# The low half of g on VectorE in the second feed-forward, and four blocks of w_out split in the last expert

## The chip, the core and the metric

The kernel runs on one NeuronCore of a Trainium2 chip. Its engines run side by side, each with an in-order queue: TensorE (PE, with weight loads as PEld), VectorE (DVE), ScalarE (ACT), GpSimd (POOL) and SyncE (SP, which issues DMAs). They wait for one another by semaphores. The metric is the device time of one execution in microseconds (us); the median of three runs of the kernel before is 1164.04 us (1163.69 to 1168.49).

## The reference

Three stages follow one another on 3072 tokens of width 384. A recurrence over time with decaying states (4 sequences, 8 heads, 768 tokens of 48 numbers a head) gives `x`. A mixture of 8 experts sends each token to the two with the largest noisy logits. The third stage, the second feed-forward, is where the change lies:

```python
def _moe2_ref(x, w_in, w_out) -> np.ndarray:
    h = x @ w_in            # 384 -> 2048
    g = h - np.tanh(h)
    return (g @ w_out).astype(np.float32)   # 2048 -> 384
```

## The kernel before

The first two stages end near 731 us of the span. The order of all instructions is written out by hand: each engine executes its own in the order in which the program issues them, and nothing moves them.

To keep precision, a matrix product is made from three: each factor is split into a high half (rounded to the type that TensorE reads, by a ScalarE copy) and a low half (the factor minus its high half), and high x high, high x low and low x high are summed in PSUM. So every operand of TensorE costs a copy and a subtraction: for `w_out` in `split_o` (L996, copy L999, subtraction L1001), for the tokens `x2h` and `x2l` in `x2_t` (L979, L980), for `g` in `split_g` (gh L1054, gl L1055).

`ff2` (L1009) takes six blocks of 512 tokens; a block is sixteen steps, one for each 128 columns of `w_in`. In step i:

- `l1` (L1022) makes h in PSUM (tile `tp`, three buffers) with nine matmuls of 512 columns. ScalarE takes t = h^2, tanh h, two shifted squares s0 and s1, and a mask m for small h (L1031 to L1039). VectorE takes s0 (L1041), s1 (L1042, reads PSUM), th = h - tanh h (L1043, reads PSUM), g from the polynomial s0 * s1 (L1044), and copies th over g where the mask says so (L1047). Between L1044 and L1047 it runs whatever waits in the list `fill`.
- `split_g` (L1050) of step i - 1: gh on ScalarE, gl on GpSimd.
- `l2` (L1060) of step i - 3 (LAG = 3): twelve matmuls of 384 columns that add g's product with a block of `w_out` into four accumulators.

Beside this, in the first five blocks, the tokens of the next block are prepared: `gather2` at f = 0, 2, 4, 6 issues two indirect DMAs on GpSimd (L951) that fetch a tile's two rows from `y_dram` into `yg`; `combine` at f = 3, 5, 7, 9 scales one on GpSimd (L961) and puts the add (L964) into `fill`; `x2_t` at f = 12, 13, 14 transposes on TensorE and splits. The tiles `yg` have two buffers each, so the third gather waits for the first add.

`w_out` has sixteen blocks of 128 rows. The first eight (NPS = 8) are split during the experts. The other eight are split in the first block of `ff2`, at f in SPLIT (L1076): the copy on ScalarE ahead of the step, the subtraction into `fill`. In the last expert (e = 7) the loop of `experts` runs its sixteen steps s with `combine` on ScalarE at s = 12 to 15 for the first four tiles, whose gathers it issues at s = 10 to 13.

Of the kernel before, what the change touches and what calls it, by code (L numbers as in the profile page):

```python
# [11 lines left out]
F32 = mybir.dt.float32  # L12
# [10 lines left out]
NT, DM = B * S, H * D          # tokens, model width  # L23
NE, FF = 8, 1024               # experts, their hidden width
FF2 = 2048
KD = DM // 128                 # 3 blocks of the model width
C = 128                        # tokens in a chunk
NCH = S // C                   # chunks of a sequence
NTILE = NT // 128
NFB, NFB2 = FF // 128, FF2 // 128  # L30
PH = 4                         # pairs of heads
HW = H * 4 * D
FILL = 512                     # slots of expert 0 that the chunks before the last fill
CAP = 832                      # slots of an expert; slot number: position * NE + expert
P_MIN = 2.0 ** -63.5
W_LO, W_HI = 0.71, 1.4         # decays whose product over a chunk stays in (2^-64, 2^64): what Ln takes

NPS = 8                        # blocks of w_out split ahead of the second feed-forward

# (h - tanh h) / h^3 = GC * ((t + GA0)^2 + GB0) * ((t + GA1)^2 + GB1) with t = h^2 <= G_T  # L40
G_T = 0.36
# [5 lines left out]
class Kernel:  # L47
# [13 lines left out]
    # ------------------------------------------------------------------ constants  # L61
    def setup(self):
        V, A, G, SP = self.V, self.A, self.G, self.SP
        dp = self.pool(self.ctx, "dram", space=bass.MemoryType.DRAM)
        self.d_dram = dp.tile([S, B * H], F32, name="d_dram")
        self.x_dram = dp.tile([NT, DM], F32, name="x_dram")      # rows: chunk, batch, token
        self.y_dram = dp.tile([NE * CAP, DM], F32, name="y_dram")
        cs = self.cs = self.pool(self.ctx, "const")
        self.ps = self.pool(self.ctx, "psum", space=bass.MemoryType.PSUM)
        self.ident = cs.tile([128, 128], F32, name="ident")  # L70
        make_identity(self.nc, self.ident)
        self.slots = cs.tile([128, NTILE, 2], I32, name="slots")
        self.mx = cs.tile([128, NTILE, 8], F32, name="mx")
        self.run = cs.tile([128, NE], F32, name="run")
        self.flag = cs.tile([128, 1], I32, name="flag")
        self.nov = cs.tile([128, NE + 1], I32, name="nov")
        self.cnt = cs.tile([128, NE], F32, name="cnt")
        self.idx = cs.tile([128, 7 * NE], F32, name="idx")
        self.ix0 = cs.tile([128, FILL // 128], I32, name="ix0")
        self.ix = cs.tile([128, 7, NE], I32, name="ix")  # L80
        self.XTT, self.XG, self.RAW = {}, {}, {}
# [4 lines left out]
    def setup_gate(self, cs):  # L86
        """What routing needs."""
        V, G, SP, I = self.V, self.G, self.SP, self.I
        self.wgn = cs.tile([128, KD, 32], F32, name="wgn")
        V.memset(self.wgn[:, :, 16:32], 0.0)  # L90
        SP.dma_start(self.wgn[:, :, 0:8], I["moe_w_gate"].rearrange("(k p) e -> p k e", p=128))
        SP.dma_start(self.wgn[:, :, 8:16], I["moe_w_noise"].rearrange("(k p) e -> p k e", p=128))
        self.noise = cs.tile([128, NTILE, NE], F32, name="noise")
        for b in range(B):
            SP.dma_start(self.noise.rearrange("p (c b) e -> p c b e", b=B)[:, :, b, :],
                         I["moe_noise"][b * S:(b + 1) * S, :].rearrange("(c p) e -> p c e", p=128))
        self.tok = cs.tile([128, NTILE], I32, name="tok")
        G.iota(self.tok, pattern=[[128, NTILE]], base=0, channel_multiplier=1)
        self.tokf = cs.tile([128, NTILE], F32, name="tokf")
        V.tensor_copy(self.tokf, self.tok)  # L100
        self.row = cs.tile([128, 128], F32, name="row")
        G.iota(self.row, pattern=[[1, 128]], base=0, channel_multiplier=0,
               allow_small_or_imprecise_dtypes=True)
        self.iota8 = cs.tile([128, NE], F32, name="iota8")
        G.iota(self.iota8, pattern=[[1, NE]], base=0, channel_multiplier=0,
               allow_small_or_imprecise_dtypes=True)
        self.ltri = cs.tile([128, 128], F32, name="ltri")
        V.tensor_scalar(self.ltri, self.jp, 0.0, None, op0=OP.is_gt)
        self.rst = cs.tile([128, NE, B + 1], F32, name="rst")
        V.memset(self.rst, 1.0)  # L110
        V.memset(self.rst[:, :, 0:1], 0.0)
        self.ones = cs.tile([128, 128], F32, name="ones")
        V.memset(self.ones, 1.0)
        self.gate_reset()

    # ------------------------------------------------------------------ routing
# [4 lines left out]
    def gate_x(self, xs, b, again):  # L121
        """x^T of a tile of tokens, and its products with both gate matrices."""
# [7 lines left out]
    def gate_mm(self):  # L130
        """Transposed logits, a batch in each quadrant."""
# [8 lines left out]
    def gate_act(self):  # L140
        """ln(1 + exp(-|z|)), its exponential made exact by its logarithm."""
# [14 lines left out]
    def gate_top(self, c):  # L156
        """One-hot rows of the two experts with the largest noisy logits."""
# [27 lines left out]
    def gate_rank(self):  # L185
        """How many earlier tokens chose each expert."""
# [6 lines left out]
    def gate_slots(self, c, oh):  # L193
        """Slots of a chunk's choices, and its part of the table of tokens by slot: a product of
        one-hot rows (slot position modulo 128) and columns (position over 128, expert)."""
# [37 lines left out]
    def gate_fill(self):  # L233
        """After the chunks before the last: the last one's tokens get no slot among the first FILL of
        expert 0, so that these are final now."""
# [9 lines left out]
    def gate(self, c, part, again=False):  # L245
        """The routing of a chunk, in eight parts."""
# [21 lines left out]
    def finish_counts(self):  # L268
        """Tokens of each expert; the tiles of tokens to look at for those with more than CAP."""
# [9 lines left out]
    # ------------------------------------------------------------------ attention  # L279
    def attention(self, ctx):  # L280
# [73 lines left out]
        def s_lay(nm, n):  # L354
            """Into tiles padded to 64 a head; of w what it lacks to W_HI, and no less than 0 (exact for
            w from W_HI / 2 on)."""
# [162 lines left out]
        def units(n, lag):  # L519
            """Where the diagonal's part of the pipeline stands: two units a step until it runs ahead."""  # L520
            m = n + lag
            return [u for u in ((2 * m, 2 * m + 1) if m < 3 else (m + 3,)) if 0 <= u < NU]
# [33 lines left out]
    def recurrence(self, ctx):  # L556
        """Attention step by step, for decays of any size, and its routing."""
# [47 lines left out]
    # ------------------------------------------------------------------ experts  # L605
    def overflow(self, ctx):
        """Tokens past CAP of an expert: each takes a slot that another expert leaves free (there
        are more slots than choices), and its row is computed here, from all tokens."""
# [49 lines left out]
        # where a tile's row for an expert goes; past the end: nowhere  # L658
# [42 lines left out]
    def conv_load(self, cv, j):  # L701
        """A block of w_in or w_out as float64 words."""
# [9 lines left out]
    def convert(self, cv, dst):  # L712
        """float64 words (low, high) of [128, 384] elements to float32, cut toward zero; below
        float32's normal range: 0."""
# [31 lines left out]
    def experts(self, ctx):  # L746
# [53 lines left out]
        def l2(e, part, f):  # L800
            """The last 64 slots take both parts of h side by side: half of its rows each."""
# [32 lines left out]
        for i in range(len(steps) + LAG):  # L834
            if i < len(steps):
# [29 lines left out]
                if e == NE - 1:  # L865
                    if s == 8:
# [32 lines left out]
    # ------------------------------------------------------------------ second feed-forward  # L899
# [26 lines left out]
    def weights(self):  # L926
        """The softmax over the two chosen logits, its maximum taken off: exp(0) and exp(l2 - l1)."""
# [17 lines left out]
    def gather2(self, i):  # L945
        """The two rows of a tile's tokens; the first chunk's lie below 512 in each expert."""
# [35 lines left out]
    def x2_first(self):  # L982
        """The first block, with the tile that comes last done last."""
# [12 lines left out]
    def split_o(self, pool, f, late=None):  # L996
        h = pool.tile([128, DM], F32R, name=f"woh{f}")
        l = pool.tile([128, DM], F32R, name=f"wol{f}")
# [10 lines left out]
    def ff2(self, ctx):  # L1009
# [12 lines left out]
        def l1(j, f):  # L1022
# [20 lines left out]
            V.tensor_tensor(th, p, th, op=OP.subtract)  # L1043
            V.scalar_tensor_tensor(g, s0, GC, s1, op0=OP.mult, op1=OP.mult)  # L1044
# [5 lines left out]
        def split_g(j, f):  # L1050
# [4 lines left out]
            G.tensor_tensor(gl, g, gh.bitcast(F32), op=OP.subtract)  # L1055
# [20 lines left out]
        SPLIT = (0, 1, 2, 4, 6, 8, 10, 11)  # L1076
        LAG = 3
        steps = [(j, f) for j in range(NB) for f in range(NFB2)]
        for i in range(len(steps) + LAG):
            if i < len(steps):  # L1080
                j, f = steps[i]
                if j == 0 and f in SPLIT:
                    self.split_o(wp, NPS + SPLIT.index(f), fill)
# [7 lines left out]
                l1(j, f)  # L1091
            if 0 < i <= len(steps):
                split_g(*steps[i - 1])
# [3 lines left out]
    # ------------------------------------------------------------------ all of it  # L1097
# [51 lines left out]
```

## Time and profile before

| what | value |
|---|---|
| median of the runs | 1164.04 us |
| profiled execution, span from first to last instruction | 1161.4 us |
| PE busy | 1084.2 us, 93% |
| DVE busy | 845.0 us, 73% |
| ACT busy | 686.2 us, 59% |
| POOL busy | 513.8 us, 44% |
| POOL gl (L1055), 96 operations | 124.5 us, 1297 ns each |
| DVE g (L1044), 96 operations | 139.5 us, 1453 ns each |

The page lists the busy time of the whole span; the stages differ, so the stretches of the second feed-forward are read apart from the rest. For the profiled execution the page gives its span only; the time of a run is measured from outside and is some 2.6 us longer than that span in the median. A matmul's end is modelled, so successive starts say more of PE than its busy share.

### The profile page before, as it was taken

What the parts mean: (1) busy time and instruction counts of PE and PEld (TensorE: products, weight loads), DVE (VectorE), ACT (ScalarE), POOL (GpSimd) and SP (SyncE); (2) the same over time, 40 slices, a digit from 0 to 9 for tenths busy, and PEclk for the clock granted to TensorE, in tenths of its full rate; (3) what the DMA queues carried; (4) which work ended last, traced back from release to release, by engine and by line L of the source; (5) the groups of instructions that cost most, each with busy time, mean ns of one, the idle gap of its engine ahead of it and who ended that gap; (6) DMA issues with size and microseconds to landing.
All of it is one profiled execution on the core that took longest, in us unless ns stands there. A gap on an engine that the chain in (4) does not pass through costs nothing. (4 is left out here: it accounts for less than half of the span.)

```text
span 1161.4 us, 18339 instructions
## 1 busy us (share of the span) xinstructions
PE 1084.2 (93%) x6540; PEld 978.8 (84%) x6541; DVE 845.0 (73%) x1562; ACT 686.2 (59%) x1316; POOL 513.8 (44%) x487
## 2 busy tenths in 40 slices
PE   3788889769999999999999999989999999999997
PEld 2677778657989898989898989778988899888896
DVE  3789898835546465646554532799999999999995
ACT  5565666332535353535343432878888888888885
POOL 4687788413133323333323202463736556363332
PEclk9898899869999999999999999999999999999999
DMA  8965452233435344444354302100202011020000
GB/s 149 160 122 116 78 103 56 69 98 99 151 115 165 101 153 134 129 130 146 114 158 135 116 22 80 54 21 14 69 1 69 15 51 32 10 73 1 28 1 27
DMA packets 116719, 97.78 MB, mean 84 GB/s; under 512 B 39432, under 2 KB 109832, under 8 KB 116616
## 3 DMA queue, kind: packets, MB, share of 16 engines
q1 hardware_dynamic: 110088, 76.82, 25.2%
q0 software_dynamic: 6528, 19.67, 5.8%
q8 instruction: 54, 0.88, 0.3%
q14 instruction: 49, 0.40, 0.1%
HBM read 76.70 MB, written 19.76 MB: 83 GB/s over the span
## 5 line engine op out<-in xcount | busy, mean ns | idle before, releaser
L794 DVE SCALAR_TENSOR_TENSOR hb<-tp,hb 128x256 fp32r<-128x256 f32 (+1 forms) x192 | 79.7, 442 | 200.4 <-ACT hb L792 193.8
L792 ACT ACTIVATE hb<-tp 128x320 fp32r<-128x320 f32 (+1 forms) x128 | 66.2, 517 | 239.3 <-PE tp L789 212.3
L1055 POOL TENSOR_TENSOR gl<-g,gh 128x512 fp32r<-128x512 f32 x96 | 124.5, 1297 | 187.5 <-ACT gh L1054 182.9
L809 PE MATMUL sc<-wh,hb 128*128 128x384 f32 x512 | 156.5, 346 | 0.0
L1044 DVE SCALAR_TENSOR_TENSOR g<-s,s 128x512 f32<-128x512 f32 x96 | 139.5, 1453 | 1.0 <-POOL gl L1055 1.0
L725 POOL TENSOR_SCALAR cvm<-cvm 128x384 f32<-128x384 f32 x32 | 40.6, 1269 | 221.1 <-ACT cvm L724 221.1
L789 PE MATMUL tp<-xh,wl 128*128 128x512 f32 (+1 forms) x384 | 135.8, 354 | 0.0
L789 PE MATMUL tp<-xl,wh 128*128 128x512 f32 (+1 forms) x384 | 135.0, 352 | 0.0
L789 PE MATMUL tp<-xh,wh 128*128 128x512 f32 (+1 forms) x384 | 134.7, 351 | 0.0
L1028 PE MATMUL tp<-x2h,wih 128*128 128x512 f32 x288 | 115.4, 401 | 1.4 <-ACTq L1117 1.4
L1028 PE MATMUL tp<-x2l,wih 128*128 128x512 f32 x288 | 114.3, 397 | 0.0
L1028 PE MATMUL tp<-x2h,wil 128*128 128x512 f32 x288 | 114.3, 397 | 0.0
L951 POOL DMA_INDIRECT yg<-y_dram,slots x48 | 57.2, 1191 | 91.0 <-DMA y_dram<-yo 56.8
L809 PEld LDWEIGHTS sc<-wh,hb 128*128 128x128 f32 x512 | 94.7, 188 | 3.2
L809 PE MATMUL sc<-wl,hb 128*128 128x384 f32 x256 | 86.4, 338 | 0.0
L1031 ACT ACTIVATE t<-tp 128x512 f32<-128x512 f32 x96 | 57.3, 597 | 42.6 <-PE tp L1028 42.1
L1047 DVE COPY_PREDICATED g<-m,th 128x512 f32<-128x512 int32 x96 | 77.1, 803 | 7.4 <-ACT s L1037 0.5
L789 PEld LDWEIGHTS tp<-xh,wl 128*128 128x128 f32 x384 | 72.2, 188 | 8.0
L789 PEld LDWEIGHTS tp<-xh,wh 128*128 128x128 f32 x384 | 72.3, 188 | 6.3 <-DVE xl L781 0.4
L789 PEld LDWEIGHTS tp<-xl,wh 128*128 128x128 f32 x384 | 72.2, 188 | 6.2
L764 DVE TENSOR_TENSOR wl<-r,wh 128x384 fp32r<-128x384 f32 x128 | 71.5, 586 | 7.3 <-ACT wh L763 7.3
L1054 ACT ACTIVATE gh<-g 128x512 fp32r<-128x512 f32 x96 | 60.5, 630 | 27.1 <-DVE g L1047 14.2
(230 smaller groups left out, 2994.3 us busy)
## 6 DMA issues: line engine op xcount, KB each, us to landing
r<-in_moe_w SPq DMA_DIRECT2D x128, 192.0 KB
y_dram<-yo SPq DMA_DIRECT2D x48, 192.0 KB
raw<-in_moe_w_in SPq DMA_DIRECT2D x16, 384.0 KB
raw<-in_moe_w_out SPq DMA_DIRECT2D x16, 384.0 KB
nv<-in_v SPq DMA_DIRECT2D x6, 768.0 KB
x_dram<-xs SPq DMA_DIRECT2D x6, 768.0 KB
out<-o SPq DMA_DIRECT2D x24, 192.0 KB
nw<-in_w SPq DMA_DIRECT2D x20, 192.0 KB
```

Source lines behind the costliest of these rows:

```text
L764: V.tensor_tensor(WL[i, f], raw, WH[i, f].bitcast(F32), op=OP.subtract)
L789: T.matmul(p[:, :n], lhsT=w[0, f][:, k, :], rhs=x[part][:, k, :], start=q == 0, stop=q == 8)
L792: A.activation(hb[:, :n], p[:, :n], AF.Relu)
L794: V.scalar_tensor_tensor(hb[:, o:o + c1 - c0], p[:, c0:c1], 0.0, hb[:, c0:c1].bitcast(F32), op0=OP.max, op1=OP.subtract)
L809: T.matmul(ACC[j][:, :DM], lhsT=h, rhs=w[1, f], start=f == 0 and i == 0, stop=f == NFB - 1 and i == len(prods) - 1)
L951: self.G.indirect_dma_start(out=y, out_offset=None, in_=rows, in_offset=bass.IndirectOffsetOnAxis(ap=self.slots[:, i, j:j + 1], axis=0))
L1028: T.matmul(p, lhsT=w[:, k, :], rhs=x[j][:, k, :], start=q == 0, stop=q == 8)
L1031: A.activation(t, p, AF.Square)
L1044: V.scalar_tensor_tensor(g, s0, GC, s1, op0=OP.mult, op1=OP.mult)
L1047: V.copy_predicated(g, m.bitcast(I32), th)
L1054: A.activation(gh, g, AF.Copy)
L1055: G.tensor_tensor(gl, g, gh.bitcast(F32), op=OP.subtract)
```

## The change

It does two things. First, gl goes from GpSimd to VectorE: `l1` takes the step before as an argument and issues its `split_g` between L1043 and L1044. Second, blocks 8 to 11 of `w_out` (NPE = 4) are split in the last expert, at s = 11 to 14, into tiles of that expert's weights for f = 0 and 1, which no later matmul reads; `ff2` splits the remaining four at f = 2, 4, 6, 8. The rest of the edit takes comments out, so later lines move by up to ten.

```diff
+NPE = 4
...
                 if e == NE - 1:
+                    if s >= 11 and s - 11 < NPE:
+                        f0, i0 = divmod(s - 11, 2)
+                        self.split_o(None, NPS + s - 11, homes=(WH[i0, f0], WL[i0, f0]))
...
-    def split_o(self, pool, f, late=None):
-        h = pool.tile([128, DM], F32R, name=f"woh{f}")
-        l = pool.tile([128, DM], F32R, name=f"wol{f}")
+    def split_o(self, pool, f, late=None, homes=None):
+        if homes is None:
+            h = pool.tile([128, DM], F32R, name=f"woh{f}")
+            l = pool.tile([128, DM], F32R, name=f"wol{f}")
+        else:
+            h, l = (x if len(x.shape) == 2 else x.rearrange("p k x -> p (k x)") for x in homes)
...
-        def l1(j, f):
+        def l1(j, f, last):
...
             V.tensor_tensor(th, p, th, op=OP.subtract)
+            if last is not None:
+                split_g(*last)
             V.scalar_tensor_tensor(g, s0, GC, s1, op0=OP.mult, op1=OP.mult)
...
-            G.tensor_tensor(gl, g, gh.bitcast(F32), op=OP.subtract)
+            V.tensor_tensor(gl, g, gh.bitcast(F32), op=OP.subtract)
...
-        SPLIT = (0, 1, 2, 4, 6, 8, 10, 11)
+        SPLIT = (2, 4, 6, 8)
...
-                    self.split_o(wp, NPS + SPLIT.index(f), fill)
+                    self.split_o(wp, NPS + NPE + SPLIT.index(f), fill)
...
-                l1(j, f)
-            if 0 < i <= len(steps):
-                split_g(*steps[i - 1])
+                l1(j, f, steps[i - 1] if i else None)
+            elif i == len(steps):
+                split_g(*steps[-1])
```

VectorE's queue in the first two steps of `ff2`, before (s0, s1, th, g, the low half wol of a block of `w_out`, the predicated copy into g):

```order
L1041 SCALAR_TENSOR_TENSOR s_9215<-s_9215,t 128x512
L1042 SCALAR_TENSOR_TENSOR s_9217<-s_9217,tp 128x512
L1043 TENSOR_TENSOR th<-tp,th 128x512
L1044 SCALAR_TENSOR_TENSOR g<-s_9215,s_9217 128x512
L1001 TENSOR_TENSOR wol_9195<-wo_7475,woh_9194 128x384
L1047 COPY_PREDICATED g<-m,th 128x512
L1041 SCALAR_TENSOR_TENSOR s_9245<-s_9245,t 128x512
L1042 SCALAR_TENSOR_TENSOR s_9247<-s_9247,tp 128x512
L1043 TENSOR_TENSOR th<-tp,th 128x512
L1044 SCALAR_TENSOR_TENSOR g<-s_9245,s_9247 128x512
L1001 TENSOR_TENSOR wol_9229<-wo_7576,woh_9228 128x384
L1047 COPY_PREDICATED g<-m,th 128x512
```

and now:

```order
L1049 SCALAR_TENSOR_TENSOR s_9220<-s_9220,t 128x512
L1050 SCALAR_TENSOR_TENSOR s_9222<-s_9222,tp 128x512
L1051 TENSOR_TENSOR th<-tp,th 128x512
L1054 SCALAR_TENSOR_TENSOR g<-s_9220,s_9222 128x512
L1057 COPY_PREDICATED g<-m,th 128x512
L1049 SCALAR_TENSOR_TENSOR s_9246<-s_9246,t 128x512
L1050 SCALAR_TENSOR_TENSOR s_9248<-s_9248,tp 128x512
L1051 TENSOR_TENSOR th<-tp,th 128x512
L1065 TENSOR_TENSOR gl<-g,gh 128x512
L1054 SCALAR_TENSOR_TENSOR g<-s_9246,s_9248 128x512
L1057 COPY_PREDICATED g<-m,th 128x512
```

The two wol are gone from these steps, and from the second step on gl of the step before stands between th and g.

POOL's queue in the first block of `ff2`, before (DMA yg: the indirect DMAs of a gather; TENSOR_SCALAR yg: the scaling of a combine):

```order
L951 DMA yg_9197<-y_dram,slots 128x384
L951 DMA yg_9199<-y_dram,slots 128x384
L1055 TENSOR_TENSOR gl<-g,gh 128x512
L951 DMA yg_9265<-y_dram,slots 128x384
L951 DMA yg_9267<-y_dram,slots 128x384
L1055 TENSOR_TENSOR gl<-g,gh 128x512
L961 TENSOR_SCALAR yg_9197<-yg_9197,wt 128x384
L1055 TENSOR_TENSOR gl<-g,gh 128x512
L951 DMA yg_9352<-y_dram,slots 128x384
L951 DMA yg_9354<-y_dram,slots 128x384
L1055 TENSOR_TENSOR gl<-g,gh 128x512
L961 TENSOR_SCALAR yg_9265<-yg_9265,wt 128x384
```

and now:

```order
L955 DMA yg_9202<-y_dram,slots 128x384
L955 DMA yg_9204<-y_dram,slots 128x384
L955 DMA yg_9265<-y_dram,slots 128x384
L955 DMA yg_9267<-y_dram,slots 128x384
L965 TENSOR_SCALAR yg_9202<-yg_9202,wt 128x384
L955 DMA yg_9352<-y_dram,slots 128x384
L955 DMA yg_9354<-y_dram,slots 128x384
L965 TENSOR_SCALAR yg_9265<-yg_9265,wt 128x384
L955 DMA yg_9447<-y_dram,slots 128x384
L955 DMA yg_9449<-y_dram,slots 128x384
L965 TENSOR_SCALAR yg_9352<-yg_9352,wt 128x384
L965 TENSOR_SCALAR yg_9447<-yg_9447,wt 128x384
```

Only gathers and scalings are left; the second tile's gather follows the first one's at once, and each later gather still follows the scaling of an earlier tile.

ScalarE's queue in the last expert, at s = 10 to 14, before (hb: the high half of h; yg: the scaling of a combine, which waits for gathered rows):

```order
L792 ACTIVATE hb<-tp 128x320 x2
L959 ACTIVATE yg_8791<-yg_8791,wt 128x384
L792 ACTIVATE hb<-tp 128x320
L959 ACTIVATE yg_8820<-yg_8820,wt 128x384
L792 ACTIVATE hb<-tp 128x320
L959 ACTIVATE yg_8849<-yg_8849,wt 128x384
L792 ACTIVATE hb<-tp 128x320
```

and now (wh: the high half of a block of `w_out`, in a place of the expert's weights):

```order
L793 ACTIVATE hb<-tp 128x320
L1006 ACTIVATE wh_0_8273<-wo_7475 128x384
L793 ACTIVATE hb<-tp 128x320
L1006 ACTIVATE wh_0_8275<-wo_7576 128x384
L963 ACTIVATE yg_8791<-yg_8791,wt 128x384
L793 ACTIVATE hb<-tp 128x320
L1006 ACTIVATE wh_1_8316<-wo_7702 128x384
L963 ACTIVATE yg_8822<-yg_8822,wt 128x384
L793 ACTIVATE hb<-tp 128x320
L1006 ACTIVATE wh_1_8318<-wo_7831 128x384
L963 ACTIVATE yg_8853<-yg_8853,wt 128x384
L793 ACTIVATE hb<-tp 128x320
```

One copy stands behind each hb from s = 10 on, three of them ahead of a scaling.

## Rows read from the trace of the kernel before

**Rows 1.** The page, part 1: busy us, share of span, instructions of each engine.

```profile
PE 1084.2 (93%) x6540; PEld 978.8 (84%) x6541; DVE 845.0 (73%) x1562; ACT 686.2 (59%) x1316; POOL 513.8 (44%) x487
```

**Rows 2.** Windows: stretch, its length, busy us per engine, granted clock, DMA share, GB/s.

```profile
768.00:773.00 5.00, 5.00 (x18) 4.43 (x18) 3.93 (x6) 1.61 (x3) 3.12 (x3) 0.66 0.02 5
...
789.00:858.10 69.10, 68.56 (x348) 61.65 (x348) 67.46 (x88) 58.20 (x104) 37.66 (x28) 1.00 0.11 35
```

**Rows 3.** Waits in 732 to 1162: who waits for whom, us, times, longest.

```profile
PE sc L1068 <- POOL gl L1055: 5.8, 5, 3.4
...
PE g L59 <- DVE x2l L980: 1.9, 5, 0.5
...
PE sc L1068 <- ACT gh L1054: 0.4, 1, 0.4
```

**Rows 4.** Timeline, 761 to 770: start us, us, engine, line, operation, [idle before].

```profile
763.24 0.67 DVE L1044 SCALAR_TENSOR_TENSOR g<-s,s 128x512 f32<-128x512 f32 x1
763.33 3.10 POOL L951 DMA_INDIRECT yg<-y_dram,slots  x1 [0.31 <-issue]
...
765.53 0.67 DVE L1042 SCALAR_TENSOR_TENSOR s<-s,tp 128x512 f32<-128x512 f32 x1
...
767.78 0.44 PE L1068 MATMUL sc<-woh,gl 128*128 128x384 f32 x1 [3.38 <-POOL gl L1055]
...
769.52 1.64 DVE L964 SCALAR_TENSOR_TENSOR x<-yg,wt,yg 128x384 f32<-128x384 f32 x1 [1.07 <-POOL yg L961]
```

**Rows 5.** Groups of DVE and POOL, 732 to 1100: count, busy us, mean ns.

```profile
L1044 DVE SCALAR_TENSOR_TENSOR g<-s,s 128x512 f32<-128x512 f32 x84 | 120.6, 1436 | 1.0 <-POOL gl L1055 1.0
...
L951 POOL DMA_INDIRECT yg<-y_dram,slots x40 | 49.4, 1236 | 31.5 <-DVE x L964 13.5 <-ACT th L1033 10.6 <-issue 5.2
L961 POOL TENSOR_SCALAR yg<-yg,wt 128x384 f32<-128x384 f32 x20 | 35.3, 1763 | 0.0
```

**Rows 6.** Timeline of the stage's start, 737 to 748.

```profile
737.53 0.68 DVE L1044 SCALAR_TENSOR_TENSOR g<-s,s 128x512 f32<-128x512 f32 x1
...
738.13 0.55 DVE L1001 TENSOR_TENSOR wol<-wo,woh 128x384 fp32r<-128x384 f32 x1
...
738.60 0.76 DVE L1047 COPY_PREDICATED g<-m,th 128x512 f32<-128x512 int32 x1
...
739.25 0.67 DVE L1041 SCALAR_TENSOR_TENSOR s<-s,t 128x512 f32<-128x512 f32 x1
...
740.01 0.63 ACT L1054 ACTIVATE gh<-g 128x512 fp32r<-128x512 f32 x1
...
742.05 0.44 PE L1068 MATMUL sc<-woh,gl 128*128 128x384 f32 x1 [0.73 <-POOL gl L1055]
...
747.36 1.05 DVE L1047 COPY_PREDICATED g<-m,th 128x512 f32<-128x512 int32 x1
```

**Rows 7.** Timeline of the last steps, 1145 to 1153.

```profile
1145.63 0.68 DVE L1041 SCALAR_TENSOR_TENSOR s<-s,t 128x512 f32<-128x512 f32 x1
...
1147.23 1.29 POOL L1055 TENSOR_TENSOR gl<-g,gh 128x512 fp32r<-128x512 f32 x1 [2.92 <-ACT gh L1054]
...
1147.42 1.65 DVE L1044 SCALAR_TENSOR_TENSOR g<-s,s 128x512 f32<-128x512 f32 x1
...
1148.57 0.44 PE L1068 MATMUL sc<-woh,gl 128*128 128x384 f32 x1 [0.36 <-POOL gl L1055]
...
1149.17 0.76 DVE L1047 COPY_PREDICATED g<-m,th 128x512 f32<-128x512 int32 x1
...
1150.02 0.63 ACT L1054 ACTIVATE gh<-g 128x512 fp32r<-128x512 f32 x1 [2.86 <-DVE g L1047]
...
1150.73 1.27 POOL L1055 TENSOR_TENSOR gl<-g,gh 128x512 fp32r<-128x512 f32 x1 [2.21 <-ACT gh L1054]
...
1152.05 0.44 PE L1068 MATMUL sc<-woh,gl 128*128 128x384 f32 x1 [0.73 <-POOL gl L1055]
```

**Rows 8.** Waits of the last expert's end, 700 to 730.

```profile
ACT yg L959 <- DMA yg<-y_dram,slots: 8.9, 4, 3.7
```

## The prediction

> **What bounds the kernel now.** I read the page's busy line first: PE is busy 93% of the span and DVE 73% [rows 1]. That mean hides the second feed-forward (the last 420 us), so I read its stretches next. From 789.00 to 858.10, one block of sixteen steps, PE is busy 68.56 of 69.10 us and DVE 67.46 [rows 2]. Both look full, so I asked the list of waits who really waits. In all of this stage PE stopped 5 times for POOL's gl, 5.8 us in total with one stop of 3.4, 5 times for VectorE's x2l, 1.9 us, and once for ScalarE's gh, 0.4 us [rows 3]. PE therefore bounds the steady blocks, and their matmuls can't be shortened by this change; what can be won is those stops and what follows from them.
>
> Where do the stops lie? Two of the five for gl are at the very end (0.36 and 0.73 us [rows 7]), the other three in the first block: 5.8 - 1.09 = 4.7 us. The largest is shown in the rows of 761 to 770 us. POOL began an indirect DMA at 763.33 and needed 3.10 us for it, where 1.24 us is the mean of the forty in this stage [rows 4, 5]; gl stood behind it in POOL's queue, and PE went on at 767.78 after 3.38 us of waiting. Then the clock fell: from 768 to 773 the granted clock was 0.66, so part of that stretch ran at the lower of PE's two levels, 1.2 instead of 2.4 GHz, behind the longest idle time of the stage [rows 2].
>
> DVE's 97% is mostly not work. Its operation g takes 1.44 us in the mean [rows 5] but 0.68 while POOL does nothing [rows 6]. The last steps show why: gl runs on POOL from 1147.23 to 1148.52, g is issued at 1147.42 and ends at 1149.07, 0.55 after gl. It sits out gl, then does its own work [rows 7].
>
> The profiled span is 1161.4 us; the median of the runs is 1164.0, so 2.6 us lie around the span. I take differences from the span and subtract them from the median.
>
> **gl on VectorE.** Removed: 96 POOL operations of about 1.3 us. Added: 96 VectorE operations of the same size. The trace has no gl on VectorE. The nearest row is g without POOL beside it, 0.68 us with two SBUF operands of the same shape [rows 6]. VectorE starts its operations faster than they last: from s0 at 1145.63 over two more to g at 1147.42 are three starts, 0.60 each [rows 7]. I take 0.60 for gl. Its lower bound is that; its upper one is 1.44, what g costs when something holds it back [rows 5].
>
> One VectorE step then is s0, s1, th and gl, 4 x 0.60; g, whose result the next operation needs, 0.68 + 0.10 (1149.07 to 1149.17 [rows 7]); and the predicated copy, 0.65 from start to start (738.60 to 739.25 [rows 6]). That is 3.83 us. A step of PE is 69.10 / 16 = 4.32 us with the transposes [rows 2]. VectorE's three x2l in a block, 0.60 each, take another 0.1 a step, so about 0.4 us is left to it where today g swallows all. A late operation in front of the copy (the combine's add or a low half of w_out) adds about 0.3: 738.13 to 738.60 is 0.47 and g's 0.78 goes down to 0.60. Such a step takes 4.12 us.
>
> **The first block.** PE runs four steps ahead at the start and then stops for gl of step 0, so nothing of VectorE's lateness is hidden there. Before: g(0) at 737.53, the low half of w_out at 738.13, the copy at 738.60, s0(1) at 739.25, PE's third product of step 0 at 742.05 [rows 6]. After: no low half here, so the copy starts at 737.53 + 0.78 = 738.31, s0(1) at 738.96, and after s0, s1 and th comes gl at 738.96 + 1.80 = 740.76, done 0.68 later at 741.44. gh is done by 740.64 even at its old place [rows 6], so gl doesn't wait for it. PE resumes about 0.55 us earlier. The two stops at the start (0.41 and 0.73) become 0.6.
>
> The other first-block stops go: 0.6 and 3.4 us. With them goes the slow clock, 5 us x 0.34 = 1.7 us [rows 2]. Lost before: 4.7 + 0.4 + 1.7 = 6.8 us.
>
> What is late next is the combine. VectorE's add waits for POOL's scaled row, and before it that row's two indirect DMAs on POOL. At 769.52 it waited 1.07 us [rows 4]. The slow DMA shows what holds them: asked at 763.33, it ended 0.90 after VectorE's s1 began at 765.53, an operation that reads PSUM; in between stood four VectorE operations with SBUF operands alone, back to back [rows 4]. After the change gl, g, a late operation, the copy and s0 make five such in a row, 3 us. Below: no add waits, 0. Above: two DMAs of 3.0 + 0.95 and one scaling of 1.8 us [rows 5] make 9.7 us where two VectorE steps give 8.2, so 1.5 for each of the second and third tile; four scalings, each holding VectorE's copy some 0.3 us as at 747.36 (1.05 against 0.76 [rows 6]); and off it the 0.5 that one step without a late operation gains on PE: 3.0 + 1.2 - 0.5 = 3.7. The DMAs' mean of 1.24 lies near the short end, so I take 1.0. First block: 6.8 - 0.6 - 1.0 = 5.2 us won. In later blocks the cover is the three steps between l1 and l2, and no stop for gl is listed there.
>
> **The transposes.** The five stops for x2l, 1.9 us [rows 3], come because x2l stands in VectorE's queue behind the copy of the step before. That copy will come 0.36 us earlier after its s0, and s0 some 0.15 earlier (both from the tail, below); the longest stop is 0.5. I take 1.8 of 1.9; below it is 0.
>
> **The tail.** Before: s0(95) at 1145.63, g at 1147.42 held until 1149.07, the copy at 1149.17, gh at 1150.02, gl 1150.73 to 1152.00, PE at 1152.05 [rows 7]. After: s0, s1, th and gl(94) take 2.40, g starts at 1148.03, the copy at 1148.81, gh at 1149.66, gl 1150.37 to 1151.05. That is 0.95, and s0 can start some 0.15 earlier without the held g ahead of it: 1.1 us.
>
> **Four splits in the last expert.** Four ScalarE copies of some 0.5 us and four VectorE subtractions of 0.55 (738.13 [rows 6]) move there. ScalarE waits in that place four times for gathered rows, 8.9 us in total [rows 8], and the copies stand in front of three of these waits, VectorE's subtractions likewise. Cost if the cover is gone: the last tile's gather ends the stage, and a subtraction that delays one indirect DMA on POOL costs up to 0.5. I take 0.2; the range is 0 to 0.5. The homes were last read by matmuls two steps earlier, so no wait comes with them. Four fewer splits in the first block are counted above.
>
> **Sum:** 5.2 + 1.8 + 1.1 - 0.2 = 7.9 us. 1164.0 - 7.9 = 1156.1.
>
> **A rule weighed.** The 3.10 us row shows an indirect DMA held while VectorE works on pairs of SBUF operands [rows 4]. The Trainium skill (SBUF — State Buffer, section SBUF: two separate sides) describes this starvation of GpSimd's DMAs for VectorE operations in a 2-port perf mode, and lets operations with two SBUF inputs block only a GpSimd operation that reads SBUF. If the latter holds for these issues, the adds aren't late, the 1.0 falls to 0.5, and the sum would be 8.4 us, 1155.6; by the row the 1.0 stands.
>
> **Rivals.** (a) The starved combine decides. VectorE waits at the adds of the second and third tile in the first block, PE stops behind it and the clock dips again. Price: 3.7 instead of 1.0, and 1.7 for the clock: 7.9 - 4.4 = 3.5, 1160.5. For it speaks the row at 763.33; against it that 40 DMAs have a mean of 1.24 us [rows 4, 5]. (b) Nothing replaces the stops: VectorE gains on PE from the first step, the 1.0 and the 0.2 are 0, and the transposes give their whole 1.9: 7.9 + 1.3 = 9.2, 1154.8. For it speaks VectorE's spare 0.4 a step; against it the eight steps with a late operation, which leave 0.2. (c) Slower: gl stands in VectorE's queue ahead of g, and if gh comes late, VectorE stands still with the copy and the next step's work behind it. It decides once the wait passes 4.32 - 3.83 = 0.49 us in each step; at 0.75 us the stage lasts 96 x 0.26 = 25 us longer and 7.9 us of gain become 17 of loss, 1181. Against it: at the start gh is done at 740.64 and gl's turn comes at 740.76.
>
> **How the numbers follow.** Forecast 0.58, (a) 0.20, (b) 0.17, (c) 0.05. Half a per cent, 5.8 us, is about what a measurement here can tell from no change. Faster by more: nearly all of the forecast (0.55), all of (b), and 0.04 of (a): 0.76. Within it: 0.03 and 0.16, and 0.01 of (c): 0.20. Slower: 0.04. The range reaches from below (b), with the bounds of the start and the tail, to (a) and a little past it, for the transposes' bound: 1152.5 to 1161.0.
>
> **What would show it.** In the changed profile: g near 0.7 us and gl on DVE near 0.7; no stop of PE above 1 us between 745 and 789, and a granted clock of 1.00 there; the first stop for gl ending near 741.5; no stops before the transposes; PE's last gl product some 1.1 us nearer to the first matmul of the last block; DVE busy about 90% in the steady blocks with gaps. The prediction fails if DVE has no gaps there, if an add waits more than 2 us, or if PE's steady block is other than 68.5 to 69 us.

## The result, and the profile after

The changed kernel takes 1155.62 us in the median of six runs (1153.47 to 1158.60), the kernel before 1164.12 us; the ratio is 0.9915 with a 95% interval of 0.9896 to 0.9934, so 8.5 us less by the medians and 9.9 by the ratio, whose interval (7.7 to 12.1 us) holds both. The forecast was 1156.1. The sum came out; two of its terms did not, and that their errors cancel is luck. The profiled execution has a span of 1156.9 us and took 1158.6.

Where the time went is read from PE's fixed points in the second feed-forward: its first matmul, the second and the third group of transposes in the first block, and the third group in the fifth block. In the kernel before (start us, us, engine, line, operation, idle time before it):

```profile
731.57 0.51 PE L1028 MATMUL tp<-x2h,wih 128*128 128x512 f32 x1 [1.35 <-ACTq L1117]
...
789.01 0.66 PE L59 MATMUL g<-ident,x 128*128 128x128 f32 x4 [0.44 <-DVE x2l L980]
...
793.70 0.60 PE L59 MATMUL g<-ident,x 128*128 128x128 f32 x4
...
1069.73 0.60 PE L59 MATMUL g<-ident,x 128*128 128x128 f32 x4
```

and after, where every line of this stage is up to ten higher:

```profile
735.27 0.51 PE L1036 MATMUL tp<-x2h,wih 128*128 128x512 f32 x1 [1.35 <-ACTq L1127]
...
788.92 1.11 PE L60 MATMUL g<-ident,x 128*128 128x128 f32 x4 [3.10 <-DVE x2l L984]
...
796.36 0.60 PE L60 MATMUL g<-ident,x 128*128 128x128 f32 x4
...
1070.39 0.60 PE L60 MATMUL g<-ident,x 128*128 128x128 f32 x4
```

With PE's last first-bank gl product (1152.05 before [rows 7], 1151.37 after) and the ends of the spans these give:

| stretch | before | after | gained | forecast |
|---|---|---|---|---|
| stage's first matmul to the first block's third transposes | 62.13 | 61.09 | 1.0 | 5.6 |
| from there to the fifth block's third transposes | 276.03 | 274.03 | 2.0 | 1.4 |
| from there to the last gl product | 82.32 | 80.98 | 1.3 | 1.1 |
| from there to the span's end | 9.35 | 5.53 | 3.8 | 0 |
| the stage | 429.83 | 421.63 | 8.2 | 8.1 |

(Of the forecast's 1.8 for the transposes, 0.4 lies in the first block.) In these two executions the stage began at 731.57 and at 735.27, so the spans differ by 4.5 only; more on that below.

The waits of the whole stage, after (who waits for whom, us, times, longest), answer to [rows 3]:

```profile
DVE s L1049 <- ACT s L1043: 22.3, 50, 3.3
...
PE g L60 <- DVE x2l L984: 3.1, 1, 3.1
...
PE sc L1078 <- DVE gl L1065: 0.8, 1, 0.8
...
DVE gl L1065 <- ACT gh L1064: 0.7, 1, 0.7
```

The five stops for gl are down to one, and VectorE, which waited 6 times for ScalarE's s0 before (4.5 us), now does so 50 times. But one stop for x2l of 3.1 us is new. g and gl cost what the forecast said, and the indirect DMAs became slower than in [rows 5] (count, busy us, mean ns of one):

```profile
L1065 DVE TENSOR_TENSOR gl<-g,gh 128x512 fp32r<-128x512 f32 x83 | 58.2, 701 | 0.0
...
L1054 DVE SCALAR_TENSOR_TENSOR g<-s,s 128x512 f32<-128x512 f32 x84 | 57.5, 684 | 0.0
...
L955 POOL DMA_INDIRECT yg<-y_dram,slots x40 | 72.8, 1821 | 214.6 <-DVE x L968 197.6 <-ACT th L1041 10.6 <-issue 6.1
```

A steady block has VectorE busy 65.30 of 68.51 us (95%, where I had said about 90). The second line is the stretch behind the new stop, at a granted clock of 0.73:

```profile
864.74:933.25 68.51, 68.51 (x350) 61.79 (x349) 65.30 (x104) 57.86 (x104) 20.08 (x12) 1.00 0.12 35
789.00:800.00 11.00, 11.00 (x45) 9.69 (x46) 8.50 (x14) 5.46 (x11) 0.00 (x0) 0.73 0.00 0
```

The new stop itself: ScalarE had x2h by 785.71, but x2l stands in VectorE's queue behind the copy of the step before, and PE's next transposes need the bank that x2l reads. They began at 788.92:

```profile
785.13 0.58 ACT L983 ACTIVATE x2h<-g 128x512 fp32r<-128x512 f32 x1
...
787.56 0.74 DVE L1057 COPY_PREDICATED g<-m,th 128x512 f32<-128x512 int32 x1
...
788.18 0.68 DVE L984 TENSOR_TENSOR x2l<-g,x2h 128x512 fp32r<-128x512 f32 x1
```

And the end. GpSimd's sequencer closes the program with a DRAIN (duration min/median/max in ns, first and last start). Before, the longest one was issued at 1150.7 behind the last gl and lasted 9.9 us, until 1160.6; after, it was issued at 1043.8 behind the last scaling of a combine, and its 11.4 us were over at 1055.2:

```profile
L1146 POOLq DRAIN  x3: 40/113/9902, 1150.7 to 1161.2; - x3
```

```profile
L1156 POOLq DRAIN  x3: 40/113/11379, 1043.8 to 1156.6; - x3
```

In both it ends 8.6 us behind the last GpSimd operation (1150.73 + 1.27 to 1160.6; 1044.06 + 2.49 to 1055.2). SyncE's waits in the last stretch, before and then after, show its weight: 4.1 us of waiting before the program's end against 0.5. The list puts this wait down to PE's queue, which had closed by 1154.1; what ended at 1160.6 is GpSimd's DRAIN.

```profile
SPq L1146 <- PEq L1146: 4.6, 2, 4.1
SPq L1146 <- DMA out<-o: 0.9, 2, 0.5
```

```profile
SPq L1156 <- DMA out<-o: 0.9, 2, 0.5
SPq L1156 <- PEq L1156: 0.7, 2, 0.5
```

### The profile page after: what moved, and what is told of

Same layout as the page of the kernel before. It is cut to its first block, busy times and chain, and to the rows that moved or that the text cites. A ratio compares the mean times of both kernels' runs of the same rounds, so it can differ in the third digit from the quotient of the medians.

```text
span 1156.9 us, 18040 instructions
## 1 busy us (share of the span) xinstructions
PE 1084.4 (94%) x6540; PEld 979.3 (85%) x6541; DVE 834.0 (72%) x1658; ACT 684.7 (59%) x1316; POOL 408.0 (35%) x391
## 5 line engine op out<-in xcount | busy, mean ns | idle before, releaser
L955 POOL DMA_INDIRECT yg<-y_dram,slots x48 | 80.6, 1679 | 274.0 <-DVE x L968 197.6
L1049 DVE SCALAR_TENSOR_TENSOR s<-s,t 128x512 f32<-128x512 f32 x96 | 68.1, 710 | 22.6 <-ACT s L1043 22.3
L1057 DVE COPY_PREDICATED g<-m,th 128x512 f32<-128x512 int32 x96 | 73.7, 768 | 2.6
L1043 ACT ACTIVATE s<-t,ga 128x512 f32<-128x512 f32 x96 | 69.9, 728 | 0.0
L1045 ACT ACTIVATE s<-t,ga 128x512 f32<-128x512 f32 x96 | 69.4, 723 | 0.0
```

Source lines behind the costliest of these rows:

```text
L955: self.G.indirect_dma_start(out=y, out_offset=None, in_=rows, in_offset=bass.IndirectOffsetOnAxis(ap=self.slots[:, i, j:j + 1], axis=0))
L1043: A.activation(s0, t, AF.Square, bias=ga[:, 0:1])
L1045: A.activation(s1, t, AF.Square, bias=ga[:, 1:2])
L1049: V.scalar_tensor_tensor(s0, s0, GB0, t, op0=OP.add, op1=OP.mult)
L1057: V.copy_predicated(g, m.bitcast(I32), th)
```

## The experiments

Theory T, from the table: the gain is 1.0 + 2.0 + 1.3 + 3.8, with the drain as its largest term, and the first block gains little because the stop moved from gl to x2l. Rival F: the forecast's own sum, with the new stop and the drain as chance.

**The changed kernel again.** No edit.

> The changed kernel once more, against the kernel before. Theory T (four terms, read from the two traces): the second feed-forward is 8.2 us shorter, made of 1.0 in the first block (the stops for gl are gone, but a stop of 3.1 us for x2l and a slow clock behind it have come), 2.0 in the later blocks, 1.3 at the last gl and 3.8 after the last product, where GpSimd's closing drain (9.9 us from its last operation's issue) no longer ends the span. Rival F (the forecast): 5.2 in the first block, 1.8 at the transposes, 1.1 at the tail; the 3.1 us stop and the 3.8 us at the end are accidents of one execution. Both: about 8 us faster. T: this profile shows the x2l stop again near the end of the first block (2.5 to 3.5 us), the granted clock below 0.8 behind it, and 5.5 us from the last gl product to the span's end. F: no stop above 1 us there, and 9 us at the end.

Ratio 0.9926 (0.9909 to 0.9944), 8.6 us less, and 7.9 by the medians. The stop is there again, and the granted clock is 0.73 in the 6.25 us behind it; the end lies 5.48 us behind the last gl product, the stage lasts 420.3.

```profile
789.77 0.66 PE L60 MATMUL g<-ident,x 128*128 128x128 f32 x4 [3.10 <-DVE x2l L984]
```

```profile
789.77:796.02 6.25, 6.25 (x26) 5.43 (x26) 4.43 (x8) 2.61 (x6) 0.00 (x0) 0.73 0.00 0
```

F's two accidents have happened twice.

**gl on VectorE alone.**

```diff
-NPE = 4
+NPE = 0
...
-        SPLIT = (2, 4, 6, 8)
+        SPLIT = (0, 1, 2, 4, 6, 8, 10, 11)
```

> gl on VectorE, but all eight blocks of w_out split in the first block as before. T: VectorE has four more low halves in the first block (0.3 us each) and two of them lie before the first copy and the second, so PE's first stop for gl is longer and VectorE later by 1.2 to 1.8 us when the transposes come; the x2l stop grows or stops for gl appear; later blocks, last gl and drain as in the changed kernel. Gain over before 5.5 to 7.5 us. F: the first block keeps about 4 of its 5.2: gain about 7. If the gain came from the splits, this kernel would be no faster than before.

Ratio 0.9944 (0.9922 to 0.9965), 6.5 us less, and 7.7 by the medians. The stop for x2l has grown from 3.1 to 4.0, by 0.9 of the 1.2 us that four low halves add to VectorE at the forecast's 0.3 each:

```profile
786.86 1.12 PE L60 MATMUL g<-ident,x 128*128 128x128 f32 x4 [3.99 <-DVE x2l L984]
```

So gl carries most of the gain (T's and F's sums lie too near each other to be told apart here), and the length of the stop follows VectorE's load.

**The splits alone.** gl on GpSimd in its old place.

```diff
-            V.tensor_tensor(gl, g, gh.bitcast(F32), op=OP.subtract)
+            G.tensor_tensor(gl, g, gh.bitcast(F32), op=OP.subtract)
...
-                l1(j, f, steps[i - 1] if i else None)
-            elif i == len(steps):
-                split_g(*steps[-1])
+                l1(j, f, None)
+            if 0 < i <= len(steps):
+                split_g(*steps[i - 1])
```

> Four blocks of w_out split in the last expert, gl on GpSimd in its old place. T and F: the transposes' stops, the held g, the last gl and (T) the drain stay as before; only the first block has four ScalarE copies and four low halves fewer, worth 0.4 us at the first stop for gl and up to 1 us later; the 3.4 us stop behind the slow indirect DMA stays or moves by a step. Gain 0 to 2 us. If the splits carried the gain: about 6 us or more.

Ratio 0.9997 (0.9981 to 1.0013): no difference. The profile has what neither theory expected: the 3.4 us stop for gl was gone, three of at most 0.7 stood in the first block, and 2.1 us for x2l:

```profile
PE g L60 <- DVE x2l L984: 2.1, 1, 2.1
PE sc L1078 <- POOL gl L1065: 2.1, 3, 0.7
```

The stage lasted 426.2 us there, 3.6 less than before, which the runs' median doesn't show; one profile of this first block doesn't stand for all.

**The last two gl on VectorE.** The kernel before otherwise; `split_g` takes the engine as an argument, GpSimd where none is named.

```diff
...
+            if last is not None:
+                split_g(*last, V)
             V.scalar_tensor_tensor(g, s0, GC, s1, op0=OP.mult, op1=OP.mult)
...
-            G.tensor_tensor(gl, g, gh.bitcast(F32), op=OP.subtract)
+            eng.tensor_tensor(gl, g, gh.bitcast(F32), op=OP.subtract)
...
-                l1(j, f)
-            if 0 < i <= len(steps):
-                split_g(*steps[i - 1])
+                l1(j, f, steps[i - 1] if i == len(steps) - 1 else None)
+            if i == len(steps):
+                split_g(*steps[-1], V)
+            elif 0 < i < len(steps) - 1:
+                split_g(*steps[i - 1])
```

> The kernel before with the gl of the last two steps alone on VectorE (in the changed kernel's place); all other gl on GpSimd. T: GpSimd's last operation ends some 8 us earlier, so its drain (8.6 us beyond that operation) is over before the outputs have landed: 3.8 us off the end, and 1.3 us at the last gl: gain 5 us, and the end of the span 5.5 us behind the last gl product as in the changed kernel. F: the last gl's 1.1 us alone, gain 1.1.

Ratio 0.9964 (0.9948 to 0.9980), 4.2 us less (4.6 by the medians) where T said 5 and F 1.1, and the interval, 2.3 to 6.1 us, leaves F out. Two operations of 96 bring about half of the change's gain. The drain is issued at 1143.8 and over at 1153.7; the span ends 5.44 us behind the last gl product:

```profile
L1150 POOLq DRAIN  x3: 40/113/9922, 1143.8 to 1157.0; - x3
```

Its first block is that of before, and here too the transposes waited for x2l:

```profile
788.31 0.66 PE L59 MATMUL g<-ident,x 128*128 128x128 f32 x4 [2.70 <-DVE x2l L980]
```

**A small GpSimd operation at the end.** The changed kernel, with a copy of one column of the last gh that nothing reads.

```diff
+        ga2 = wp.tile([128, 1], F32, name="ga2")
...
+            if (j, f) == steps[-1]:
+                G.tensor_copy(ga2, gh.bitcast(F32)[:, 0:1])
             GT[j, f] = gh, gl
```

> The changed kernel with one small GpSimd operation more: a copy of one column of the last gh, which nothing reads. It costs no engine of the chain any time. Theory T (GpSimd's closing drain lasts 8.6 us beyond its last operation, whenever that was, and ended the span of the kernel before): the drain is issued near the last gh and ends the span again; 3 to 4.5 us slower than the changed kernel, the span ending 9 to 10 us behind the last gl product. Rival (the 3.8 us came from the heavy gl operations near the end, or by chance): no change.

Ratio to before 0.9942 (0.9924 to 0.9961). In the profile the mechanism is as T has it: the copy runs beside gl, and the span ends 9.38 us behind the last gl product instead of 5.53, 3.85 more.

```profile
1146.41 0.70 POOL L1068 COPY ga<-gh 128x1 f32<-128x1 f32 x1 [102.86 <-ACT gh L1065]
...
1147.12 0.44 PE L1081 MATMUL sc<-woh,gl 128*128 128x384 f32 x1
```

```profile
L1159 POOLq DRAIN  x3: 40/113/9321, 1146.4 to 1156.3; - x3
```

8.6 us lie once more between the end of the copy (1147.11) and that of the drain (1146.4 + 9.3 = 1155.7); an operation of one column holds the end as gl did. The ratios say 1.9 to 3.1 us slower than the changed kernel (0.9942 against 0.9926 and 0.9915), mostly less than T's 3 to 4.5, and with these intervals not far from nothing: the end is shown by the profile, not by the time of the runs. In the profiled execution the clock behind the x2l stop stayed at 1.00, which returned 1.5 to 2.7 us in the same span:

```profile
788.74:793.45 4.71, 4.71 (x25) 4.27 (x26) 4.45 (x8) 2.62 (x6) 0.00 (x0) 1.00 0.00 0
```

**TensorE no longer waits for x2l.** The changed kernel, with ScalarE copying the bank.

```diff
         self.A.activation(self.X2H[j][:, k, :], pc, AF.Copy)
-        self.V.tensor_tensor(self.X2L[j][:, k, :], pc, self.X2H[j][:, k, :].bitcast(F32), op=OP.subtract)
+        xs = self.fx.tile([128, 512], F32, name="xs", bufs=3)
+        self.A.activation(xs, pc, AF.Copy)
+        self.V.tensor_tensor(self.X2L[j][:, k, :], xs, self.X2H[j][:, k, :].bitcast(F32), op=OP.subtract)
```

> The changed kernel with another way for the low half of the next block's tokens: ScalarE copies the bank of the transposes to SBUF behind the high half, VectorE subtracts from that copy (three buffers), so TensorE waits for ScalarE alone and not for VectorE. Theory T (the first block's stop moved from gl to x2l because VectorE stays 3 us behind TensorE there, and the slow clock behind it costs another 2 to 3 us): the stop of 3.1 us and the slow clock go; the stage lasts 415 to 417 us instead of 420 to 422, 4 to 6.5 us faster than the changed kernel. Rival N (VectorE's lateness has to be paid somewhere): a stop for gl or for a bank of h of about the same length takes its place, gain below 1.5 us.

1150.53 us in the median; ratio 0.9882 (0.9863 to 0.9901), 13.7 us less than before (12.2 by the medians), and by the ratios 3.8 to 5.1 less than the changed kernel: the low end of T's 4 to 6.5, not N's 1.5. The stage lasts 415.7. The transposes wait 0.43 for ScalarE's copy, and the granted clock is 1.00 behind them:

```profile
784.53 0.66 PE L60 MATMUL g<-ident,x 128*128 128x128 f32 x4 [0.43 <-ACT xs L985]
```

```profile
784.53:789.23 4.70, 4.70 (x25) 4.26 (x26) 4.67 (x9) 4.70 (x10) 0.00 (x0) 1.00 0.00 0
789.23:800.00 10.77, 10.77 (x56) 9.58 (x55) 10.67 (x18) 10.24 (x20) 0.00 (x0) 1.00 0.01 2
```

VectorE's lateness had only to be kept off the one bank; no stop for gl came in its place. This version beats both kernels.

**The kernel before again.**

> The kernel before once more, for a second profile. If the 3.4 us stop for gl behind the 3.1 us DMA and the slow clock belong to the kernel, they stand in this profile too and the stage lasts 429 to 431 us; if they are one execution's, this first block is 2 to 4 us shorter (the kernel of the last two gl, whose first block is that of before, had a longest stop of 0.6 for gl there). The drain: 9.9 us from its issue, ending the span, in both cases.

One profile: the stage lasts 429.3 us, the end is 9.39 behind the last gl product, and the long stop is there, two steps earlier than in [rows 4], behind a DMA of 3.11 us:

```profile
754.30 3.11 POOL L951 DMA_INDIRECT yg<-y_dram,slots  x1 [0.30 <-issue]
...
758.76 0.69 PE L1068 MATMUL sc<-woh,gl 128*128 128x384 f32 x1 [3.34 <-POOL gl L1055]
```

So it belongs to the kernel, at a place that varies; in the two other profiles with gl on GpSimd (the splits alone, the last two gl) it was absent, and x2l stopped PE for 2.1 and 2.7 us instead.

## Why the prediction was right, and where it was wrong

**The steady blocks: right.** gl on VectorE starts every 0.60 us and lasts 0.70 in the mean, g fell from 1.44 to 0.68, and the wait that rival (c) needed is absent: VectorE waited for gh once, at the very end, 0.7 us. The four later blocks won 2.0 where the forecast has 1.4; their stops for x2l are listed no more. The experiments put it down to gl: this stretch lasts 273.1 to 274.0 us in all five profiles with gl on VectorE, with or without the splits, and 275.5 to 276.5 in the four with gl on GpSimd there.

**The tail: right.** 1.3 against 1.1, by the steps of the forecast: g is no longer held, and each piece from the copy to gl follows sooner than in [rows 7]:

```profile
1146.03 0.69 DVE L1049 SCALAR_TENSOR_TENSOR s<-s,t 128x512 f32<-128x512 f32 x1 [0.29 <-ACT s L1043]
...
1148.44 0.69 DVE L1054 SCALAR_TENSOR_TENSOR g<-s,s 128x512 f32<-128x512 f32 x1
...
1149.16 0.76 DVE L1057 COPY_PREDICATED g<-m,th 128x512 f32<-128x512 int32 x1
...
1149.96 0.63 ACT L1064 ACTIVATE gh<-g 128x512 fp32r<-128x512 f32 x1 [2.22 <-DVE g L1057]
...
1150.62 0.69 DVE L1065 TENSOR_TENSOR gl<-g,gh 128x512 fp32r<-128x512 f32 x1 [0.70 <-ACT gh L1064]
...
1151.37 0.44 PE L1078 MATMUL sc<-woh,gl 128*128 128x384 f32 x1
```

**The first stop: direction right, size off.** 0.55 us were forecast, 0.3 came (10.48 us behind the stage's first matmul before, 10.15 after). gl took 0.90 instead of 0.68, while GpSimd, free of gl, scaled the first row of the combine (744.23), long before its add. The 0.3 per scaling was about right; that one of them would meet the first gl was not foreseen.

```profile
742.68 0.67 DVE L1049 SCALAR_TENSOR_TENSOR s<-s,t 128x512 f32<-128x512 f32 x1
...
744.23 1.28 POOL L965 TENSOR_SCALAR yg<-yg,wt 128x384 f32<-128x384 f32 x1
...
744.47 0.90 DVE L1065 TENSOR_TENSOR gl<-g,gh 128x512 fp32r<-128x512 f32 x1
...
745.42 0.44 PE L1078 MATMUL sc<-woh,gl 128*128 128x384 f32 x1 [0.83 <-DVE gl L1065]
```

**"First block: 6.8 - 0.6 - 1.0 = 5.2 us won": wrong.** Counting the clock behind the stop it won 1.0. The failed step is "no stops before the transposes": I had x2l's stops vanish because VectorE's step gets shorter. In the first block it never gets the chance. VectorE is behind from the start, runs steps of mostly 4.0 to 4.2 us with the combine's adds and the splits (4.4 and 4.8 in two where GpSimd's scalings ran beside gl), and has no gap from 739.4 to 792. While gl was late, PE stopped for gl and so came later to the transposes; with these stops gone, PE arrives earlier and VectorE's lateness shows at the next place where PE needs it, x2l. The wait of 0.44 that it had there became 3.1, and the slow clock, which I had removed, came behind that stop instead. The experiments with ScalarE's copy (stop and slow clock gone, about 4 to 5 us) and with four more low halves (stop 0.9 longer) show it. The first blocks give the price: from the stage's first matmul to the third transposes it is 55.5 us with ScalarE's copy, 58.2 with the stop and the clock at 1.00 (the added copy), 59.8 and 61.1 with the stop and the slow clock (the changed kernel twice). So the stop costs 2.7 and the slow clock 1.6 to 2.9. The kernel before has 62.1 and 61.1 there: the 1.0 is that of one pair of executions, and without the stop the first block wins the forecast's 5.6 or more.

**The 1.0 for late adds: wrong in its place.** No add waited for its scaling. The DMAs were starved as the first part of rival (a) has it, and more than before: 1.82 us in the mean, up to 3.75. One asked at 756.83 ended 0.94 behind the start of s1 at 759.63, with five VectorE operations on SBUF operands in a row ahead of it, as in [rows 4]:

```profile
756.74 0.69 DVE L1065 TENSOR_TENSOR gl<-g,gh 128x512 fp32r<-128x512 f32 x1
756.83 3.74 POOL L955 DMA_INDIRECT yg<-y_dram,slots  x1 [0.30 <-issue]
...
759.04 0.70 DVE L1049 SCALAR_TENSOR_TENSOR s<-s,t 128x512 f32<-128x512 f32 x1
...
759.63 0.70 DVE L1050 SCALAR_TENSOR_TENSOR s<-s,tp 128x512 f32<-128x512 f32 x1
```

But only gathers and scalings stand in GpSimd's queue now, and no engine waited for them. The Trainium skill (SBUF — State Buffer, section SBUF: two separate sides) names operations in a 2-port perf mode for such starvation; here it stands beside operations with two SBUF inputs, and the trace decides. No run took the pairs away from beside a DMA, so the cause itself is read from the order in time, not shown by an edit.

**GpSimd's drain: missing.** 3.8 us of the gain are in no step of the forecast. "2.6 us lie around the span" ended my look at the end, though the span runs 7 us past the last copy of an output. (The 2.6 was wrong too: every run listed with both has 1.7 to 1.8 us between its span and its time; the rest is the difference between executions.) The last two gl alone (4.2 us, of which its tail gives 1.1) and the added copy (3.85 us at the end of its span) show this term, and all nine profiles agree: the span ends 9.35 to 9.40 us behind the last gl product in the four where GpSimd still works near the end, 5.44 to 5.53 in the five others.

**The four splits: right, with one point open.** Alone they change nothing that can be measured, and beside gl on VectorE they save 1.3 to 2.6 us of the stage (422.9 without them, 421.6 and 420.3 with them, one profile each). Their cost in the last expert, 0.2 in the forecast, is lost in the spread: from the experts' first matmul to the stage's first lie 475.3 to 476.7 us with them and 475.1 to 476.3 without. In the four profiles with both parts the stage began at 733.7 to 736.3, in the five others at 731.6 to 733.0. The difference is there already where the experts begin (258.4 to 259.6 against 255.4 to 257.7), behind the attention, whose instructions are the same, and the granted clock steps at other moments in it. The splits lie far behind that place, and the splits alone began at 731.7. What shifts the clock there stays open. In each of those four kernels the profiled run was also the longest of its runs, so the late start need not be in the others; the medians show a gain of the stage's size.

## What to carry to other kernels

When a stop of the bounding engine is removed, ask at which other places that engine waits for the same late producer, and in what order it reaches them; the lateness is not gone but moves to the next one. Look at what closes the program: an engine that needs microseconds to drain should finish its last operation early, even if another engine must take that work. A bank that two engines must read before it is free is best emptied by the one with time to spare.

## What the runs showed of the hardware that was not expected

- GpSimd's closing DRAIN ends 8.6 us behind its last operation, whether that was a subtraction of 128x512, a scaling 110 us before the end, or a copy of one column.
- Behind a stop of PE of 2.7 to 4.0 us the granted clock fell to between 0.59 and 0.73 until the third transposes in four profiles, and stayed at 1.00 in one (a stop of 3.1).
- An indirect DMA on GpSimd took 0.94 to 3.82 us to issue. Thirteen in the nine profiles took 3.1 us or more, and each ended 0.89 to 0.96 us behind the start of an s1, VectorE's first operation that reads PSUM behind a row of operations on SBUF.
